# First head's maxima turned ahead of the second pair's bits, fewer fillers, and a new order table, in an attention and soft-mixture kernel

## The chip, the core and the metric

The kernel runs on one core of a Trainium2 chip. The core has five engines that work side by side, each with a queue of its own that is served strictly in order: TensorE (PE in the profile) multiplies matrices, VectorE (DVE), ScalarE (ACT) and GpSimd (POOL) work on elements, and SyncE (SP) issues transfers, which 16 DMA engines carry out. Engines wait for one another through semaphores. The metric is the device time of one execution in microseconds (us), less is better.

## The reference

Inputs are `q`, `k`, `v` of 4 batches x 8 heads x 768 tokens x 64 and a projection `proj` (64x6). Each token gets six sign bits for q and six for k; a query sees only the keys with the same six bits. The attention output goes through a soft mixture of experts.

```python
q_bits = (np.einsum('bhsd,dk->bhsk', q, proj) > 0)
k_bits = (np.einsum('bhsd,dk->bhsk', k, proj) > 0)
mask = q_bucket[:, :, :, None] == k_bucket[:, :, None, :]
scores = np.where(mask, scale * q @ k.T, -1e9)
attn = exp(scores - max(scores)); attn = attn / (sum(attn) + 1e-9)
x = (attn @ v) as 3072 tokens x 512
...
logits = x @ phi
slot_input = softmax(logits over tokens).T @ x      # 32 slots
slot_out[e] = relu(slot_input[e] @ w1[e]) @ w2[e]   # 8 experts
out = softmax(logits over slots) @ slot_out
```

## The kernel before

There are 32 heads of 768 tokens, so six tiles of 128 rows each; two heads share a batch of loads and are called a pair. For one head h the kernel does this:

- `load` brings the raw q and k of a pair into the buffer `raw` (there is one such buffer, so the next pair's load waits until all readers of the last are through). `bits` multiplies `raw` with the projection on PE, and `over` (L598) turns the products into bit rows `bt`.
- `split_hi` (ACT, L564) and `split_lo` (L568) split `raw` into a rounded part and a rest, in the buffer `w4` (`w` in the profile); for the first two pairs `split_lo` runs on POOL, later on DVE.
- `spread_y`, `spread_bits`, `spread_l` and `spread_x` bring these into one of three operand buffers `XY` by DMAs (L572) or casts (L581). Heads 0, 3, 6... use `XY_141`, heads 1, 4... `XY_142`, heads 2, 5... `XY_143`. Rows 64 to 95 of each start out as constants, zeros and ones, that `first_y` writes once.
- `smax` (L650) makes the products from which a row's maximum is taken, in banks of 512 columns; there are two such banks. `most` (L660, L663, DVE) reduces one; nine reductions make a head. `shift` (L671 to L674, DVE) makes a shift of the maximum, and `shift_rows` turns it into a row of `XY`: for head 0 by products with the identity (L685) and casts on ACT and DVE (L687, L688), for all others by a product (L691), a cast (`mr`, L694) and a DMA.
- `scores` (L706) makes the masked, shifted scores with two products, in three banks; `exps` (L712, ACT) takes the exponential of a bank, again nine to a head; `acc` (L720, L723, POOL) sums the exponentials, and `av` (L732) multiplies them with `v`.

For each pair, sums, reciprocals (`pair_rec`, L751) and the logits of the mixture (`pair_add`, L771 and L773) follow; for each batch of eight heads a running softmax (`batch_...`); and at the end two layers of experts, whose weights are loaded along the way.

`keep_warm` (L524) issues PE products that nothing reads, called fillers here. While head 0's maxima are made, `smax` issues two fillers behind each bank's last product, and eight behind the very last.

**Order.** The kernel is scheduled by hand: instructions go into each engine's queue in the order in which the program issues them. The program makes a list of steps, each with a number, sorts it and issues it. One unit of the number is one of a head's six tiles. `WHEN` has the numbers of a head in the middle, relative to the head's start; `FIRST` replaces single numbers for the first heads, and `LAST` for the last ones. So a change of these numbers moves steps on all engines at once, SP's transfers too.

Of the kernel before, what the change touches and what calls it, by code (L numbers as in the profile page):

```python
# [45 lines left out]
WHEN = {'load': -21.2267,  # L46
 'bits': -13.66,
 'split_hi': -13.5002,
 'split_lo': [-12.4984, -11.5982],
 'spread': [[-13.2693, -9.5764, -8.868, -8.1927], [-12.8094, -12.4762, -10.6553, -10.2703]],  # L50
 'load_v': [0.2058, -0.1243],
 'smax': [[-8.5643, -8.5079, -8.2213, -6.4622, -6.9729, -7.4688, -7.2277, -5.9816, -5.6736, -4.4691, -4.4083, -4.9056], [-9.6301, -9.6119, -8.9294, -8.8703, -8.072, -5.8278, -5.6254, -7.7717, -5.8098, -3.9059, -3.8333, -4.928]],
 'scores': [[0.2222, 3.1567, 4.6188, 0.8581, 0.0933, 2.3238, 2.8345, 2.9849, 4.1596, 3.8243, 4.4451, 2.0185], [0.1374, 0.8796, 1.1366, 0.6129, 2.7988, 0.7436, 1.4189, 1.4936, 3.1041, 3.407, 3.5317, 3.2581]],
 'shift': [-3.0973, -3.6413],
 'shift_rows': [-2.9069, -2.4936],
 'acc': [[5.6492, 5.6716, 7.3725, 7.9438, 13.0472], [4.136, 4.6871, 7.6692, 9.1593, 9.1679]],
 'av': [[8.0639, 8.1163, 8.2235, 8.2342, 8.2455, 8.2853], [4.6384, 5.3911, 5.4621, 5.4695, 5.5104, 5.8666]],
 'pair_sum': 17.1288,
 'pair_turn': 17.6253,
 'pair_rec': [19.1149, 18.8822, 18.8381],  # L60
 'pair_log': 17.2824,
 'pair_x': [20.0505, 21.5752],
 'pair_add': 19.4108,
 'batch_both': 20.004,
 'batch_max': 22.2214,
 'batch_exp': 22.9038,
 'batch_turn': 27.3524,
 'batch_scale': 26.8147,
 'batch_slots': 28.9459,
 'batch_weigh': 28.16,  # L70
 'batch_share': 28.3581,
 'batch_arrange': 31.3938,
 'load_weights': 20.0463,
 'most': [[-8.202, -8.0525, -6.4306, -6.7445, -6.9514, -5.8288, -5.3798, -3.6478, -4.8148], [-8.9354, -8.7621, -8.4274, -6.309, -4.4576, -7.5104, -5.212, -3.7625, -3.8958]],
 'exps': [[1.1938, 4.8483, 2.6209, 0.9684, 2.85, 3.0592, 6.3758, 5.1251, 2.7028], [0.621, 1.687, 1.3077, 3.163, 2.7312, 1.8054, 4.0071, 4.3752, 4.1145]]}

FIRST = {('load', 4): 4.5756,
 ('bits', 2): -9.2469,
 ('split_hi', 2): -4.1215,
 ('split_lo', 2, 0): -1.8302,  # L80
 ('split_lo', 2, 1): -1.4643,
 ('spread_y', 2): -0.7103,
 ('spread_bits', 2): -1.5968,
 ('spread_l', 2): 0.3263,
 ('spread_x', 2): 1.0892,
 ('smax', 1, 0, 0): -9.1254,
 ('smax', 1, 0, 1): -11.3828,
 ('smax', 1, 1, 0): -11.2936,
 ('smax', 1, 1, 1): -8.0143,
 ('smax', 1, 2, 0): -3.7459,  # L90
 ('smax', 1, 2, 1): -1.1988,
 ('smax', 1, 3, 0): -0.1767,
 ('smax', 1, 3, 1): -4.9113,
 ('smax', 1, 4, 0): -2.3094,
 ('smax', 1, 4, 1): -1.6126,
 ('smax', 1, 5, 0): -1.3265,
 ('smax', 1, 5, 1): -5.1589,
 ('first_y', 1): -25.6577,
 ('first_y', 2): -82.8016,
 ('spread_y', 1): -28.42,  # L100
 ('spread_l', 0): -16.9491,
 ('spread_bits', 1): -17.4347,
 ('bits_rest',): -25.7325,
 ('bits_copy',): -42.5516,
 ('most', 1, 0): -5.0585,
 ('most', 1, 2): -8.9264,
 ('most', 1, 3): -6.9825,
 ('most', 1, 4): -2.1518,
 ('most', 1, 6): 1.0699,
 ('most', 1, 7): -3.1409,  # L110
 ('most', 1, 8): -1.7431,
 ('most', 1, 10): 1.8611,
 ('most', 1, 11): -3.8479,
 ('bits_first', 1): -27.9402,
 ('bits', 0): -58.4653,
 ('split_hi', 0): -52.0505,
 ('split_lo', 0, 0): -26.6142,
 ('split_lo', 0, 1): -17.7524,
 ('spread_x', 0): -8.8883,
 ('load_v', 0): -5.7992,  # L120
 ('smax', 0, 0, 0): -36.0223,
 ('scores', 0, 0, 0): -7.0811,
 ('most', 0, 0): -25.23,
 ('exps', 0, 0): -6.0662,
 ('smax', 0, 0, 1): -24.9204,
 ('scores', 0, 0, 1): -3.7252,
 ('smax', 0, 1, 0): -19.0895,
 ('scores', 0, 1, 0): -3.5002,
 ('most', 0, 2): -18.6614,
 ('exps', 0, 2): -1.9816,  # L130
 ('smax', 0, 1, 1): -31.0234,
 ('scores', 0, 1, 1): -5.6082,
 ('most', 0, 3): -28.5477,
 ('exps', 0, 3): -4.5302,
 ('smax', 0, 2, 0): -27.4878,
 ('scores', 0, 2, 0): -7.1428,
 ('most', 0, 4): -24.8444,
 ('exps', 0, 4): -6.2104,
 ('smax', 0, 2, 1): -17.8184,
 ('scores', 0, 2, 1): -0.679,  # L140
 ('smax', 0, 3, 0): -16.4261,
 ('scores', 0, 3, 0): -0.1673,
 ('most', 0, 6): -14.5291,
 ('exps', 0, 6): 0.9718,
 ('smax', 0, 3, 1): -19.0487,
 ('scores', 0, 3, 1): -1.6999,
 ('most', 0, 7): -18.5753,
 ('exps', 0, 7): 1.9975,
 ('smax', 0, 4, 0): -18.101,
 ('scores', 0, 4, 0): 1.7338,  # L150
 ('most', 0, 8): -15.938,
 ('exps', 0, 8): 2.9611,
 ('smax', 0, 4, 1): -13.4653,
 ('scores', 0, 4, 1): -1.7121,
 ('smax', 0, 5, 0): -13.1733,
 ('scores', 0, 5, 0): -1.2017,
 ('most', 0, 10): -10.3631,
 ('exps', 0, 10): -1.1195,
 ('smax', 0, 5, 1): -15.1162,
 ('scores', 0, 5, 1): 0.7755,  # L160
 ('most', 0, 11): -13.5877,
 ('exps', 0, 11): 1.6535,
 ('shift', 0): -9.6249,
# [1 line left out]
 ('av', 0, 0): -0.6783,
 ('acc', 0, 1): -0.9262,
 ('av', 0, 1): 1.2278,
 ('acc', 0, 2): 4.1542,
 ('av', 0, 2): 2.8888,
 ('acc', 0, 3): 4.7925,  # L170
 ('av', 0, 3): 3.1606,
 ('acc', 0, 4): 8.0454,
 ('av', 0, 4): 3.9777,
 ('acc', 0, 5): 12.7489,
 ('av', 0, 5): 4.9168,
 ('spread_l', 1): -11.2081,
 ('spread_x', 1): -8.261,
 ('load_v', 1): -37.7236,
 ('scores', 1, 0, 0): 4.5898,
 ('exps', 1, 0): 5.0814,  # L180
 ('scores', 1, 0, 1): 4.9999,
 ('scores', 1, 1, 0): 5.0209,
 ('exps', 1, 2): 5.0485,
 ('scores', 1, 1, 1): 6.5311,
 ('exps', 1, 3): 7.2738,
 ('scores', 1, 2, 0): 4.0108,
 ('exps', 1, 4): 4.1108,
 ('scores', 1, 2, 1): 6.1313,
 ('scores', 1, 3, 0): 7.5354,
 ('exps', 1, 6): 8.8956,  # L190
 ('scores', 1, 3, 1): 5.4113,
 ('exps', 1, 7): 6.4461,
 ('scores', 1, 4, 0): 6.0575,
 ('exps', 1, 8): 6.4808,
 ('scores', 1, 4, 1): 8.5523,
 ('scores', 1, 5, 0): 8.5825,
 ('exps', 1, 10): 10.3343,
 ('scores', 1, 5, 1): 7.7148,
 ('exps', 1, 11): 9.4405,
 ('shift', 1): 1.9079,  # L200
 ('shift_rows', 1): 2.3524,
 ('av', 1, 0): 9.2796,
 ('acc', 1, 1): 10.1366,
 ('av', 1, 1): 10.7972,
 ('acc', 1, 2): 12.4825,
 ('av', 1, 2): 10.8292,
 ('acc', 1, 3): 13.171,
 ('av', 1, 3): 10.9443,
 ('acc', 1, 4): 16.6799,
 ('av', 1, 4): 11.0367,  # L210
 ('acc', 1, 5): 16.9021,
 ('av', 1, 5): 14.2599,
# [1 line left out]
 ('load_v', 2): 12.3045,
 ('smax', 2, 0, 0): 2.0338,
 ('scores', 2, 0, 0): 11.7331,
 ('most', 2, 0): 2.5309,
 ('exps', 2, 0): 12.2527,
 ('smax', 2, 0, 1): 2.9954,
 ('scores', 2, 0, 1): 15.6262,  # L220
 ('smax', 2, 1, 0): 3.2113,
 ('scores', 2, 1, 0): 15.9257,
 ('most', 2, 2): 3.5357,
 ('exps', 2, 2): 16.5105,
 ('smax', 2, 1, 1): 5.2006,
 ('scores', 2, 1, 1): 11.4302,
 ('most', 2, 3): 5.4198,
 ('exps', 2, 3): 11.7998,
 ('smax', 2, 2, 0): 5.9106,
 ('scores', 2, 2, 0): 12.2138,  # L230
 ('most', 2, 4): 6.2178,
 ('exps', 2, 4): 13.3874,
 ('smax', 2, 2, 1): 2.2592,
 ('scores', 2, 2, 1): 11.5015,
 ('smax', 2, 3, 0): 2.2693,
 ('scores', 2, 3, 0): 11.909,
 ('most', 2, 6): 4.3309,
 ('exps', 2, 6): 13.1304,
 ('smax', 2, 3, 1): 4.5227,
 ('scores', 2, 3, 1): 12.3863,  # L240
 ('most', 2, 7): 4.8456,
 ('exps', 2, 7): 13.5581,
 ('smax', 2, 4, 0): 4.6005,
 ('scores', 2, 4, 0): 16.3303,
 ('most', 2, 8): 4.8433,
 ('exps', 2, 8): 18.3449,
 ('smax', 2, 4, 1): 5.2697,
 ('scores', 2, 4, 1): 14.4321,
 ('smax', 2, 5, 0): 5.5095,
 ('scores', 2, 5, 0): 16.1037,  # L250
 ('most', 2, 10): 6.7902,
 ('exps', 2, 10): 17.4702,
 ('smax', 2, 5, 1): 7.0394,
 ('scores', 2, 5, 1): 13.4048,
 ('most', 2, 11): 7.2001,
 ('exps', 2, 11): 14.0731,
 ('shift', 2): 7.353,
 ('shift_rows', 2): 8.5764,
 ('spread_y', 3): 3.2798,
 ('spread_bits', 3): 5.3768,  # L260
 ('spread_l', 3): 6.0304,
 ('spread_x', 3): 6.6527}
# [1020 lines left out]
```

## Time and profile before

| | us |
|---|---|
| median of three runs | 495.46 |
| lowest and highest run | 493.95, 496.46 |
| the profiled execution, its own time | 495.47 |
| its span, from the first to the last instruction | 493.7 |
| PE busy | 477.1 |
| DVE busy | 358.4 |
| POOL busy | 335.0 |
| ACT busy | 264.2 |

The profile lists busy time by engine, groups of instructions by source line, the chain of work that ended last (followed back from the last instruction to what released each step), and the instructions in order of time. "Idle before <- releaser" names what ended an engine's wait. The ends of PE's products are modelled, so PE can show as busy while it in fact waits a little; how long a product really takes in a stream is best read from the chain of waits, where each piece starts when the one before it ends.

### The profile page before, as it was taken

The page shows a single profiled execution, that of the slowest core. Times are in us where ns is not written, and L with a number is a line of the kernel's source. Part 1 is how long each engine was busy: PE and PEld are TensorE (multiplying, and loading weights), DVE is VectorE, ACT ScalarE, POOL GpSimd, SP SyncE. Part 2 cuts the span into 40 slices and gives each one's busy share as a digit, 9 for nine tenths or more (in the row PEclk, how much of TensorE's full clock was granted, in tenths as well). Part 3 has the DMA queues.
Part 4 walks back from the last instruction along what each step waited for, and adds up shares of the span by engine and source line. Part 5 has one row for each costly group of instructions (what it writes and reads, how often), then busy time and mean ns, then how long its engine had stood idle before and what let it go on. Part 6 is the DMA issues. An engine that isn't in the chain of part 4 may idle for free.

```text
span 493.7 us, 8863 instructions
## 1 busy us (share of the span) xinstructions
PE 477.1 (97%) x3182; PEld 294.1 (60%) x3182; DVE 358.4 (73%) x669; ACT 264.2 (54%) x506; POOL 335.0 (68%) x205
## 2 busy tenths in 40 slices
...
GB/s 157 179 82 184 98 156 110 191 159 180 176 183 172 168 172 147 198 154 192 154 194 148 170 166 189 166 191 165 189 165 102 63 173 244 245 406 394 413 313 282
DMA packets 37455, 93.66 MB, mean 190 GB/s; under 512 B 7058, under 2 KB 13332, under 8 KB 37412
## 3 DMA queue, kind: packets, MB, share of 16 engines
...
q10 hardware_dynamic: 100, 0.08, 0.1%
q0 software_dynamic: 32, 0.07, 0.0%
HBM read 52.76 MB, written 6.29 MB: 120 GB/s over the span
## 4 chain that ended last, share of the span: by engine, by line
PE 89%; DMA 3%; DVE 3%; POOL 1%; issue 1%; ACT 1%; DVEq 0%; SPq 0%; ACTq 0%; POOLq 0%
PE st L706 27%; PE av L732 26%; PE smx L650 14%; PE qs L1211 3%; PE qh L1160 3%; PE mi L605 3%; PE mi L744 2%; PE mi L759 2%; PE mi L794 2%; DMA raw<-qk 2%; DMA XY<-w 1%; PE mi L943 1%; PE mi L779 1%; PE mi L691 1%; PE st L810 1%
## 5 line engine op out<-in xcount | busy, mean ns | idle before, releaser
L723 POOL TENSOR_TENSOR acc<-acc,pt 128x768 f32<-128x768 f32 x125 | 245.0, 1970 | 35.5 <-ACT pt L712 29.7
L712 ACT ACTIVATE pt<-st 128x512 f32<-128x512 f32 x288 | 162.6, 594 | 56.7 <-PE st L706 54.2
L706 PE MATMUL st<-XY 128*128 128x512 f32 (+1 forms) x768 | 171.0, 343 | 0.5 <-DVE XY L688 0.5
L663 DVE TENSOR_REDUCE mx<-smx 128x1 f32<-128x512 f32 x192 | 128.5, 678 | 37.7 <-PE smx L650 34.9
L706 PEld LDWEIGHTS st<-XY 128*128 128x128 f32 x768 | 120.4, 189 | 25.7 <-issue 9.6
L732 PE MATMUL av<-pt,v 128*64 128x384 f32 x768 | 133.1, 491 | 0.0
L650 PE MATMUL smx<-XY 96*128 96x512 f32 (+1 forms) x384 | 120.7, 364 | 2.8 <-DVE mx L663 2.4
L650 PEld LDWEIGHTS smx<-XY 96*128 96x128 f32 x384 | 68.2, 189 | 40.6 <-DVE mx L663 17.6
L732 PEld LDWEIGHTS av<-pt,v 128*64 128x64 f32 x768 | 51.5, 136 | 67.9 <-issue 65.3
L720 POOL TENSOR_TENSOR acc<-pt 128x768 f32<-128x768 f32 x32 | 58.3, 1821 | 33.8 <-ACT pt L712 33.6
L660 DVE TENSOR_REDUCE mx<-smx 128x2 f32<-128x512 f32 x96 | 65.6, 685 | 11.3 <-PE smx L650 10.9
L736 ACT COPY avs<-av 128x384 f32<-128x384 f32 x32 | 15.3, 479 | 83.0 <-PE av L732 83.0
L568 DVE TENSOR_TENSOR w<-raw,w 128x768 fp32r<-128x768 f32 x28 | 43.0, 1535 | 0.6 <-ACT w L564 0.6
L751 DVE RECIPROCAL sm<-sm 128x128 f32<-128x128 f32 x45 | 38.4, 909 | 0.0
L564 ACT CAST w<-raw 128x768 fp32r<-128x768 f32 x32 | 25.0, 830 | 3.2 <-DMA XY<-w 2.3
L796 DVE TENSOR_TENSOR xq<-mi,r 128x256 f32<-128x256 f32 x45 | 17.6, 419 | 10.0 <-PE mi L794 10.0
L581 ACT CAST XY<-w 64x768 fp32r<-64x768 f32 x30 | 23.5, 830 | 0.0
L598 DVE TENSOR_SCALAR bt<-mi,con 128x384 fp32r<-128x384 f32 x15 | 10.2, 677 | 13.9 <-PE mi L605 7.6
L605 PE MATMUL mi<-raw,pb 128*32 128x384 f32 x128 | 16.2, 518 | 1.1 <-DMA raw<-qk 1.1
L568 POOL TENSOR_TENSOR w<-raw,w 128x768 fp32r<-128x768 f32 x4 | 7.2, 1821 | 13.7 <-ACT w L564 12.2
L794 PE MATMUL mi<-ident,avs 128*128 128x128 f32 x90 | 14.7, 272 | 0.0
L1211 PE MATMUL qs<-w 128*32 128x256 f32 x232 | 14.6, 380 | 0.0
(168 smaller groups left out, 330.6 us busy)
## 6 DMA issues: line engine op xcount, KB each, us to landing
...
XY<-w SPq DMA_DIRECT2D x48, 384.0 KB
raw<-qk SPq DMA_DIRECT2D x32, 384.0 KB
...
```

The lines of the kernel that those rows point to most:

```text
L568: (nc.vector if h > 2 else nc.gpsimd).tensor_tensor(out=w[:, 2 * x + 1], in0=st[h]["raw"][:, x], in1=w[:, 2 * x], op=ALU.subtract)
L605: nc.tensor.matmul(pts_b[j // 2 if h == 0 else 0][32 * j:32 * j + 32, 0:HC], pb[:, 32 * (j // 2):32 * (j // 2) + 32], st[h]["raw"][:, j // ...
L650: nc.tensor.matmul(pt[:, o:o + b - a], s["Y"][0:96, 0, t * P:(t + 1) * P], s["Y"][0:96, 1, a:b], start=True, stop=True)
L660: nc.vector.tensor_reduce(out=mx[:, n - 1:n + 1], in_=s["sm_ps", n - 1].rearrange("p (a x) -> p a x", a=2), axis=AX.X, op=ALU.max)
L663: nc.vector.reduce_max(out=mx[:, n:n + 1], in_=s["sm_ps", n], axis=AX.X)
L706: nc.tensor.matmul(pt[:, o:o + b - a], x[:, 1, i * P:(i + 1) * P], x[:, 0, a:b], start=first, stop=not first)
L712: nc.scalar.activation(s["P", n // 4][:, 512 * u:512 * u + 512], s["st_ps", n - (n % 4 == 2)], AF.Exp, scale=D ** -0.5)
L720: nc.gpsimd.tensor_tensor(out=s["acc"], in0=pr[:, 0:S], in1=pr[:, S:2 * S], op=ALU.add)
L723: eng.tensor_tensor(out=s["acc"], in0=s["acc"], in1=pr[:, a * S:(a + 1) * S], op=ALU.add)
L732: nc.tensor.matmul(s["av"][64 * c:64 * c + 64, 0:HC], s["v"][:, i, :], pr[:, o + c * HC:o + (c + 1) * HC], start=(i == 0), stop=(i == NT - 1))
L751: nc.vector.reciprocal(out=rs[:, k * P:(k + 1) * P], in_=rs[:, k * P:(k + 1) * P])
L1211: nc.tensor.matmul(po[32 * j:32 * j + 32], hTs[g][:, f, 32 * j:32 * j + 32], wt[1, x, 2 * g + f // 4, j][:, (f % 4) * HM:(f % 4 + 1) * HM] ...
```

## The change

Three things are changed.

1. `first_y(1)`, the constant rows of `XY_142`, is written by two ACT copies from a broadcast column in place of two POOL memsets.
2. While head 0's maxima are made, one filler follows each bank in place of two, and the eight behind the last product become one, with five more issued by a step of their own.
3. All numbers of `WHEN`, `FIRST` and `LAST` are new. Among them: `shift_rows(0)` now comes ahead of `bits(2)`, the bits of the second pair, and the second pair's `load` comes behind `spread_x(0)`.

The number of PE products that are not fillers stays the same.

```diff
     def first_y(i):
         for x in range(2):
-            nc.gpsimd.memset(XYs[i][64:96, x].bitcast(F32), float(x))
+            dst = XYs[i][64:96, x].rearrange("p a s -> p (a s)")
+            if i == 1:
+                nc.scalar.copy(dst, (ones if x else mz_wide)[64:96, 0:1].broadcast_to([32, 2 * S]))
+            else:
+                nc.gpsimd.memset(dst.bitcast(F32), float(x))
...
         if h == 0:
-            s["smax"] = s.get("smax", 0) + 1
-            keep_warm(8 if s["smax"] == 2 * NT else 2 * (n % 4 != 1), True)
+            if n % 4 != 1:
+                keep_warm(1, True)
...
+    at(-11.05, keep_warm, 5, True)
...
- ('bits', 2): -9.2469,
+ ('bits', 2): -7.8765,
...
- ('shift_rows', 0): -8.2597,
+ ('shift_rows', 0): -10.4942,
...
- ('load', 2): -9.5805,
+ ('load', 2): -19.4862,
```

Line numbers of the changed kernel are 4 higher from `first_y` on. Three places show what the tables do.

**PE, from the end of head 0's maxima to head 0's first scores.** `smx<-XY_142` are maxima of head 1, `mi<-raw,pb` the bits of the second pair, `mi<-ident,mz` and `st<-ident,mz` the turning of head 0's row, `st<-XY_141` head 0's scores, `av<-pt_83,ones` fillers. Before:

```order
L524 MATMUL av<-pt_83,ones 32x128 x8
L650 MATMUL smx<-XY_142 128x256 x2
L605 MATMUL mi<-raw,pb 32x384 x4
L650 MATMUL smx<-XY_142 128x512
L685 MATMUL mi<-ident,mz 33x128 x4
L685 MATMUL st<-ident,mz 33x128 x2
L650 MATMUL smx<-XY_142 128x512
L706 MATMUL st<-XY_141 128x512 x6
```

And of the change:

```order
L524 MATMUL av<-pt_83,ones 32x128 x6
L689 MATMUL mi<-ident,mz 33x128 x4
L689 MATMUL st<-ident,mz 33x128 x2
L654 MATMUL smx<-XY_142 128x512
L710 MATMUL st<-XY_141 128x512 x2
L654 MATMUL smx<-XY_142 128x512
L710 MATMUL st<-XY_141 128x256 x4
L654 MATMUL smx<-XY_142 128x512
L710 MATMUL st<-XY_141 128x512 x2
L654 MATMUL smx<-XY_142 128x256
L609 MATMUL mi<-raw,pb 32x384 x4
```

The bits, which need the second pair's load, stood ahead of the turning; now four pairs of score products stand between, and the bits come later.

**POOL, from its memsets at the start to the second pair.** `w<-raw,w` is `split_lo`, `bt<-pt_81` the first pair's bit rows, `XY_142` the constant rows of change 1. Before:

```order
L568 TENSOR_TENSOR w_168<-raw,w_168 128x768
L598 TENSOR_SCALAR bt<-pt_81,con 128x384
L548 MEMSET XY_142 32x1536 x2
L568 TENSOR_TENSOR w_168<-raw,w_168 128x768
L541 CAST ident<-pt_82 128x128
```

And of the change:

```order
L572 TENSOR_TENSOR w_149<-raw,w_149 128x768 x2
L602 TENSOR_SCALAR bt<-pt_81,con 128x384
L541 CAST ident<-pt_82 128x128
L544 TENSOR_TENSOR pairs<-ident 128x64
L572 TENSOR_TENSOR w_332<-raw,w_332 128x768 x2
```

Both halves of the first pair's rest now come ahead of the bit rows, and the memsets are gone. On ACT the two copies of change 1 stand ahead of the two copies of head 0's bits (`bits_copy`, L625 before) that POOL's bit rows are made from.

**SP, around the second pair's load** (`raw<-qk`); `XY_141<-w` brings the operands of head 0, `XY_142<-w` those of head 1. Before:

```order
L572 DMA XY_142<-w_168 64x2x768
L572 DMA XY_141<-w_168 32x2x768
L572 DMA XY_142<-w_168 32x2x768
L471 DMA raw<-qk 128x768 x2
L572 DMA XY_141<-w_168 64x2x768
```

And of the change:

```order
L576 DMA XY_142<-w_149 64x2x768
L576 DMA XY_141<-w_149 32x2x768
L576 DMA XY_141<-w_149 64x2x768
L576 DMA XY_141<-w_149 32x2x768
L471 DMA raw<-qk 128x768 x2
L576 DMA XY_142<-w_149 32x2x768
```

Two transfers of head 0's operands (`spread_x(0)`) moved ahead of the load, and one of head 1's behind it.

In the middle of the kernel the order of PE stays nearly the same. On DVE, `pair_add` (before: L771, L773) moved from just ahead of a `shift` to just behind it.

More of the change, by code (lines that the diff above doesn't have):

```diff
@@ L43 @@
 C_ALL = C_FD + P
[L46 to L75, printed above, removed]
@@ L77 @@
-FIRST = {('load', 4): 4.5756,
- ('bits', 2): -9.2469,
[L79 to L163, printed above, removed]
- ('shift_rows', 0): -8.2597,
[L165 to L212, printed above, removed]
- ('load', 2): -9.5805,
[L214 to L262, printed above, removed]
```

453 lines of the change are left out of this document (333 added, 120 removed).

## The prediction

> **What bounds the kernel now.** I read first the busy time of the engines in stretches of the span (columns: stretch, its length, then busy time and number of instructions for PE, weight loads, DVE, ACT, POOL, then the clock granted to PE, DMA share, GB/s).
>
> ```profile
> 0.00:25.35 25.35, 21.79 (x124) 13.57 (x124) 12.48 (x26) 6.30 (x10) 14.06 (x15) 1.00 0.65 168
> 25.35:56.20 30.85, 28.95 (x145) 17.09 (x146) 21.50 (x34) 18.99 (x34) 22.42 (x12) 1.00 0.44 106
> 56.20:425.00 368.80, 368.80 (x2299) 229.54 (x2298) 299.33 (x548) 220.34 (x417) 292.83 (x172) 1.00 0.61 170
> ```
>
> From 56.2 to 425 us PE is busy without a gap, at full clock, and the change takes no useful product away. There a new order can add waits but hardly remove any. What can be won lies ahead of 56.2 us, where PE runs fillers and waits. So I read the chain of waits there (start, length, what ran).
>
> ```profile
> 9.41 1.65 POOL bt L598
> ...
> 11.12 2.70 POOL XY L548 x2
> ...
> 13.89 1.81 POOL w L568
> ...
> 15.95 0.11 SPq L471
> ...
> 16.11 5.55 DMA raw<-qk
> ...
> 21.70 0.84 PE mi L605 x4
> ...
> 22.97 1.01 PE mi L685 x8
> ...
> 25.35 1.66 PE st L706 x6
> ```
>
> It reads: POOL makes bit rows, memsets, then `split_lo`; only then is `raw` free and the second pair's load can go; PE stands at its bits until 21.70; behind them in the queue stand the turning of head 0's row (22.97) and its scores, which begin at 25.35. But head 0's shift was ready long before, as DVE's instructions in order of time show:
>
> ```profile
> 11.11 0.67 DVE L598 TENSOR_SCALAR XY<-mi,con 16x384 fp32r<-16x384 f32 x1
> ...
> 14.06 0.69 DVE L663 TENSOR_REDUCE mx<-smx 128x1 f32<-128x512 f32 x1 [0.29 <-PE smx L650]
> ...
> 18.00 0.69 DVE L660 TENSOR_REDUCE mx<-smx 128x2 f32<-128x512 f32 x1 [0.30 <-PE smx L650]
> ...
> 19.20 0.17 DVE L674 SCALAR_TENSOR_TENSOR mz<-mi,mz 128x6 f32<-128x6 f32 x1
> ```
>
> The last reduction ends at 18.69 and the shift at 19.37, 0.7 later. From 14.06 to 18.00 there are five reductions, each behind a wait of 0.3 for PE: a bank costs (18.00 - 14.06)/4 = 0.98, of which 0.69 is the reduction.
>
> **Term 1: head 0's scores start earlier.** What fills that 0.3 are the fillers:
>
> ```profile
> 13.95 0.62 PE L524 MATMUL av<-pt,ones 128*32 128x128 f32 x4
> ```
>
> Two fillers are 4 products and 0.62; one is 0.31. A bank then costs 0.69 and DVE sets the pace; five waits of 0.3 are about 1.5 saved. Against this stands the first edit: two ACT copies come ahead of the copies for the bit rows.
>
> ```profile
> 5.79 0.83 ACT L562 CAST XY<-raw 64x768 fp32r<-64x768 f32 x1 [0.39 <-DMA raw<-qk]
> 6.53 1.56 ACT L564 CAST w<-raw 128x768 fp32r<-128x768 f32 x2
> 8.00 0.47 ACT L625 COPY pt<-mi 64x384 f32<-64x384 f32 x1
> ```
>
> A copy of 768 columns takes 0.83, one of 384 takes 0.47; none of 1536 is in the trace. It takes no less than 0.83 and no more than 2 x 0.83 = 1.66; by the slope, 0.83 + 2 x 0.36 = 1.55, which I take, as the nearest to these rows. The two end at 6.53 + 1.56 + 3.1 = 11.2, the next copy at 11.7, and the last bits of head 0 on DVE, which wait for that copy, end near 12.35 (before: 11.11 + 0.67 = 11.78), though now with three of the nine reductions ahead of them and not one. Six remain: 0.5 until the next product is there, 6 x 0.69 = 4.1, and some 0.6 where a bank of two halves must be filled first, 17.6; the shift's 0.6 makes 18.2. At the bounds of the copy this is 16.8 and 18.4. Six fillers (1.9) run in that time and cost nothing: PE has nothing else to do until the shift is there. From the turning to the first score it took 25.35 - 22.97 = 2.4. So the first score comes at 18.2 + 2.4 = **20.6, 4.7 earlier**.
>
> What could be late in its stead? Head 0's operands are issued near 11.3, when POOL ends its second half (9.4 + 1.81), and have 9 us to land. Head 1's bit rows come later: POOL makes them from 12.2 to 13.9 (1.65), so ACT's four transfers start at 13.9 in place of 12.53.
>
> ```profile
> 12.53 3.81 ACTq L572 DMA_DIRECT2D XY<-bt  x4
> ```
>
> ```profile
> 19.75 0.51 PE L650 MATMUL smx<-XY 96*128 96x256 f32 x2
> ```
>
> They take at most 3.81, to 17.7; before, they ended at 16.34 and the first product that needs them ran at 19.75 without a wait, so they land within 3.4 of the last issue, now at 21.1 at the worst: a wait of 0 to 0.5, and I take 0. ACT is free for the turning's cast at 17.7. The second pair's load goes behind two transfers more (near 1 each to issue, by 3.81/4), at about 13.2. It took 15.95 to 21.66, 5.7; the two ahead of it are 384 and, for half the rows, 192 KB, which at the 220 GB/s of this stretch are 2.6 more:
>
> ```profile
> 19.75:25.35 5.60, 4.39 (x25) 2.19 (x24) 2.02 (x4) 0.84 (x2) 0.00 (x0) 1.00 0.98 220
> ```
>
> ```profile
> XY<-w SPq DMA_DIRECT2D x48, 384.0 KB
> ```
>
> So it lands at 21.5 at the latest; its bits stand behind 2 us of products that begin at 20.6, at 22.6.
>
> **Term 2: what PE still owes.** What products take in a stream, from the chain in the middle of the kernel:
>
> ```profile
> 72.19 0.24 PE smx L650
> ...
> 74.06 0.78 PE mi L605 x8
> 74.84 4.02 PE av L732 x24
> ...
> 80.46 0.46 PE st L706 x2
> ```
>
> 512 columns are 0.235, 256 about 0.12; a tile of `av` is 4.02/6 = 0.67. Head 1's first score is here:
>
> ```profile
> 37.61 0.73 PE L706 MATMUL st<-XY 128*128 128x512 f32 x2
> ```
>
> From 25.35 to 37.61 PE's queue holds head 0's scores (6 x 0.47 + 6 x 0.24 = 4.2), eight products of head 1's maxima (1.4), five of head 2's (0.7), a turning (0.1) and five tiles of `av` (3.4): 9.8 of work in 12.26, so 2.4 are lost. The same chain shows where:
>
> ```profile
> 27.28 0.70 DVE mx L663
> ...
> 30.80 0.80 PE av L732 x4
> ```
>
> PE waits 27.0 to 28.0 for a bank, and products cost more where kinds alternate (an `av` tile alone 0.80). In the changed order the same stretch holds 12.2: the bits (0.8) and half a us of maxima that before ran ahead of 25.35 (together 1.25), and 1.15 that before ran behind 37.61. The 1.25 must be paid; the 1.15 comes back. With the same loss of 2.4, head 1's first score comes at 20.6 + 12.2 + 2.4 = 35.2, and the gain is 4.7 - 1.25 = 3.45, **3.4**. The loss is the unknown. Without it the gain would be 5.8. It can also grow: in the changed order on ACT, the four casts of the second pair follow one another, where now they stand two and two among the exponentials:
>
> ```profile
> 27.62 1.58 ACT L564 CAST w<-raw 128x768 fp32r<-128x768 f32 x2
> ...
> 30.98 1.55 ACT L581 CAST XY<-w 64x768 fp32r<-64x768 f32 x2
> ```
>
> For 3.1 us no score bank comes free; three banks hold 1.4 of scores, and maxima and an `av` tile lie beside them (about 1.7), so the block costs 0 to 2. I take the loss of before, as the one that was measured.
>
> For the rest I take nothing: the middle keeps nearly its old order on PE, whose full queue hides any step moved on another engine (the price if not is the third rival's), and at the end a turning of expert shares moves into a stretch where PE waits anyway. The profiled execution took 495.47 (its span 493.70, 1.77 around it), beside the median of 495.46; less 3.4 makes **492.1**.
>
> **Rivals.** *The wait moves downstream* (chance 0.23): the block on ACT costs 1 to 2, or POOL, whose sums stand behind the same splits, frees a buffer late. The gain is 0 to 2.4: 493.1 to 495.5. For it: ACT's casts can't shrink. Against it: they start earlier by 3.
>
> *The lost time shrinks too* (0.11): more independent products in the queue fill the 2.4: 489.7.
>
> *The clock drops* (0.04). PE's last product ends at 484.8:
>
> ```profile
> 484.00:485.00 1.00, 0.78 (x6) 0.53 (x4) 1.00 (x2) 1.00 (x3) 0.00 (x0) 1.00 1.01 401
> ...
> 488.00:489.00 1.00, 0.00 (x0) 0.00 (x0) 0.00 (x0) 0.00 (x0) 0.00 (x0) 0.66 1.01 401
> 489.00:490.00 1.00, 0.00 (x0) 0.00 (x0) 0.00 (x0) 0.00 (x0) 0.00 (x0) 0.50 1.03 414
> ```
>
> The clock halves near 488.3, after 3.5 us of idleness, and no wait of the new start is longer than 1.5. If a low share of busy time were enough, head 0's twelve maxima would double at the worst, by 4.5 (busy time of the maxima alone, same columns without POOL):
>
> ```profile
> 8.89:18.00 9.11, 4.47 (x12) 1.97 (x12) 5.43 (x9) 0.00 (x0) 1.00 0.53 133
> ```
>
> That gives 496.6, within 0.5%. The Trainium skill ("TensorE: Matmul & The Clock Gate", "Part 1: The HAM clock gate") says that the gate falls to half rate after an idle window of about 3.4 us, which speaks against taking fillers away; this trace agrees with the 3.5, and by that rule the clock stays up here.
>
> *DVE becomes the bound in the middle* (0.07), the one that ends slower. Before, DVE has a gap there, and a bank is free ahead of its use:
>
> ```profile
> 197.96 0.69 DVE L663 TENSOR_REDUCE mx<-smx 128x1 f32<-128x512 f32 x1 [0.42 <-PE smx L650]
> ```
>
> ```profile
> 199.04 0.40 PE L650 MATMUL smx<-XY 96*128 96x512 f32 x1
> ```
>
> `pair_add` now stands between the shift and this reduction. The sum of DVE's work ahead of it stays, and I find DVE through by about 197.9, still in time. The slack is 0.42 and 199.04 - 198.65, together 0.8. If DVE came later by more, each of 15 pairs would pay the excess; from 3.4/15 = 0.23 on, the kernel is slower than before. At half a us: 492.1 + 7.5 = 499.6.
>
> *The change does not do what it says* (0.03): the load lands well after 22.6 or head 0's operands after 20.6, and PE stands where it stood: 495.5.
>
> **How the numbers follow.** The forecast, a gain of 2.5 to 5, has 0.52. A measurement of this kernel can tell about 0.5%, here 2.5 us, from no change. Faster: 0.52 + 0.11 = 0.63. Within 0.5%: 0.23 + 0.04 + 0.03 = 0.30. Slower: 0.07. The range 489.3 to 495.2 leaves out the clock and DVE, half of the last rival, and some of the first two, 0.19 in all.
>
> **What would show it.** Right: the reductions of head 0 stand 0.7 apart, the shift ends near 18.2, the first score comes near 20.6, the second pair's load is issued near 13, head 1's first score comes near 35.2, and PE has no gaps from some 53 us on. Wrong: a score that waits for operands at 21, losses between 20.6 and 35 of much more than 2.4, a granted clock below 1, or gaps on PE in every pair.

## The result and the profile after

The change makes the kernel slower: 502.27 us median of four runs (501.85 to 502.48) against 495.19 for the kernel before beside it (493.95 to 496.46). The ratio is 1.0151, 95% interval 1.0125 to 1.0176. The profiled execution's span is 500.3, 6.6 more than before. I had expected 3.4 less, so 10.0 us are to be found. Medians and ratios leave out two executions in a slower state, one of e6 (664.82) and one of the kernel before beside e9 to e12 (2636.97).

The page of the changed kernel, its span, the granted clock in 40 slices of 12.5 us, and the first line of the chain:

```profile
span 500.3 us, 8836 instructions
...
PEclk9599999999999999999999999999999999989997
...
PE 85%; DVE 7%; DMA 3%; issue 1%; ACT 1%; POOL 0%; DVEq 0%; SPq 0%; ACTq 0%
```

And of the kernel before:

```profile
PEclk9999999999999999999999999999999999999997
...
PE 89%; DMA 3%; DVE 3%; POOL 1%; issue 1%; ACT 1%; DVEq 0%; SPq 0%; ACTq 0%; POOLq 0%
```

Before, the clock row had a 9 everywhere but in the last slice. Now there is a 5 in the second slice and an 8 near 440 us, and DVE has 7% of the chain where it had 3%. The first and the third of the stretches that opened the prediction, of the changed kernel:

```profile
0.00:25.35 25.35, 22.34 (x95) 13.11 (x96) 11.42 (x25) 9.34 (x12) 11.35 (x13) 0.80 0.66 169
...
56.20:425.00 368.80, 365.30 (x2265) 225.91 (x2263) 308.74 (x542) 214.50 (x413) 289.82 (x170) 1.00 0.60 165
```

In the first the clock is 0.80 where it was 1.00; in the other PE idles for 3.5 us (368.80 - 365.30), where it had no gap.

**An account by progress.** ACT copies each head's product when its last `av` is done, so the starts of these 32 copies are milestones that both kernels share. Those of heads 2 and 29, in the instructions in order of time, before:

```profile
70.53 0.48 ACT L736 COPY avs<-av 128x384 f32<-128x384 f32 x1 [4.06 <-PE av L732]
...
409.38 0.48 ACT L736 COPY avs<-av 128x384 f32<-128x384 f32 x1 [4.06 <-PE av L732]
```

And after:

```profile
71.45 0.48 ACT L740 COPY avs<-av 128x384 f32<-128x384 f32 x1 [2.94 <-PE av L736]
...
414.51 0.48 ACT L740 COPY avs<-av 128x384 f32<-128x384 f32 x1 [3.50 <-PE av L736]
```

The changed kernel is 0.92 behind at head 2 and 5.13 behind at head 29. Between, the distance stands still or shrinks by some 0.02 a head, except for three steps, at heads 10, 18 and 26, of 1.47, 1.64 and 1.66. A last milestone is the turning of the expert shares by `fold`, before and after:

```profile
445.11 1.13 PE L1141 MATMUL mi<-fold,run_x 128*128 128x128 f32 x8 [0.30 <-DVE run_x L948]
```

```profile
452.12 1.13 PE L1146 MATMUL mi<-fold,run_x 128*128 128x128 f32 x8 [0.47 <-DVE run_x L952]
```

That is 7.01 behind; from there to the end 0.4 come back. Against the prediction of 3.4 ahead, the 10.0 are: **4.3 at the start** (0.92 + 3.4), **4.2 in the middle** (5.13 - 0.92), and **1.5 at the end** (6.6 - 5.13).

**The start.** PE in order of time, after (`av<-pt,ones` are fillers, two products to each):

```profile
10.42 0.49 PE L654 MATMUL smx<-XY 96*128 96x512 f32 x1
10.84 0.41 PE L524 MATMUL av<-pt,ones 128*32 128x128 f32 x2
11.18 0.38 PE L654 MATMUL smx<-XY 96*128 96x256 f32 x1
12.40 0.50 PE L654 MATMUL smx<-XY 96*128 96x512 f32 x1 [0.84 <-DVE XY L602]
12.84 0.41 PE L524 MATMUL av<-pt,ones 128*32 128x128 f32 x2
13.17 0.38 PE L654 MATMUL smx<-XY 96*128 96x256 f32 x1
13.48 0.41 PE L524 MATMUL av<-pt,ones 128*32 128x128 f32 x2
13.82 1.32 PE L654 MATMUL smx<-XY 96*128 96x256 f32 x3
...
18.00 0.80 PE L654 MATMUL smx<-XY 96*128 96x512 f32 x1
18.73 3.03 PE L524 MATMUL av<-pt,ones 128*32 128x128 f32 x12
21.69 1.92 PE L689 MATMUL mi<-ident,mz 128*33 128x128 f32 x8
...
25.00 0.73 PE L710 MATMUL st<-XY 128*128 128x512 f32 x2 [0.24 <-DVE XY L692]
```

From 13.82 on a product takes longer: a maximum's 512 columns 0.80 and not 0.50, eight products of the turning 1.92 and not 1.06 as before and in e7. Six fillers now last 3.03, and the turning stands behind them. The first score comes at 25.00, 0.35 ahead of before where 4.7 was expected.

### The profile page after: what moved, and what is told of

It reads as the page before. It is cut to its first block, busy times and chain, and to the rows that moved or that the text cites. A ratio compares the mean times of both kernels' runs of the same rounds, so it can differ in the third digit from the quotient of the medians.

```text
span 500.3 us, 8836 instructions
## 1 busy us (share of the span) xinstructions
PE 482.1 (96%) x3162; PEld 294.0 (59%) x3162; DVE 369.4 (74%) x669; ACT 264.0 (53%) x508; POOL 332.0 (66%) x203
## 4 chain that ended last, share of the span: by engine, by line
PE 85%; DVE 7%; DMA 3%; issue 1%; ACT 1%; POOL 0%; DVEq 0%; SPq 0%; ACTq 0%
PE st L710 26%; PE av L736 24%; PE smx L654 15%; PE qs L1216 3%; PE qh L1165 3%; DVE w L572 3%; PE mi L609 2%; PE mi L763 2%; PE mi L748 2%; PE mi L798 2%; DVE mx L667 1%; DMA XY<-mr 1%; PE mi L783 1%; PE mi L947 1%; PE mi L695 1%
## 5 line engine op out<-in xcount | busy, mean ns | idle before, releaser
L716 ACT ACTIVATE pt<-st 128x512 f32<-128x512 f32 x288 | 158.2, 595 | 73.8 <-PE st L710 72.3
L710 PE MATMUL st<-XY 128*128 128x256 f32 (+1 forms) x768 | 170.5, 343 | 0.5 <-DVE XY L692 0.2
L710 PEld LDWEIGHTS st<-XY 128*128 128x128 f32 x768 | 118.2, 189 | 17.7 <-ACT pt L716 2.7
L654 PEld LDWEIGHTS smx<-XY 96*128 96x128 f32 x384 | 65.9, 191 | 45.5 <-issue 21.6
L664 DVE TENSOR_REDUCE mx<-smx 128x2 f32<-128x512 f32 x96 | 64.8, 678 | 11.8 <-PE smx L654 10.9
L572 DVE TENSOR_TENSOR w<-raw,w 128x768 fp32r<-128x768 f32 x28 | 52.8, 1886 | 0.3 <-ACT w L568 0.2
L755 DVE RECIPROCAL sm<-sm 128x128 f32<-128x128 f32 x45 | 40.4, 926 | 0.0
L572 POOL TENSOR_TENSOR w<-raw,w 128x768 fp32r<-128x768 f32 x4 | 7.2, 1821 | 18.2 <-DMA XY<-bt 16.6
L698 ACT CAST mr<-mi 12x128 fp32r<-12x128 f32 x31 | 7.9, 254 | 16.7 <-PE mi L695 13.8
L748 PE MATMUL mi<-acc,ones 128*32 128x384 f32 x120 | 15.2, 497 | 0.0
```

The lines of the kernel that those rows point to most:

```text
L572: (nc.vector if h > 2 else nc.gpsimd).tensor_tensor(out=w[:, 2 * x + 1], in0=st[h]["raw"][:, x], in1=w[:, 2 * x], op=ALU.subtract)
L654: nc.tensor.matmul(pt[:, o:o + b - a], s["Y"][0:96, 0, t * P:(t + 1) * P], s["Y"][0:96, 1, a:b], start=True, stop=True)
L664: nc.vector.tensor_reduce(out=mx[:, n - 1:n + 1], in_=s["sm_ps", n - 1].rearrange("p (a x) -> p a x", a=2), axis=AX.X, op=ALU.max)
L710: nc.tensor.matmul(pt[:, o:o + b - a], x[:, 1, i * P:(i + 1) * P], x[:, 0, a:b], start=first, stop=not first)
L716: nc.scalar.activation(s["P", n // 4][:, 512 * u:512 * u + 512], s["st_ps", n - (n % 4 == 2)], AF.Exp, scale=D ** -0.5)
L748: nc.tensor.matmul(pt[r:r + 32, 0:HC], ones, st[h + a]["acc"][:, c * HC:(c + 1) * HC], start=True, stop=True)
```

## The experiments

The kernels that were run, by the milestones of their profiled executions (heads: against 70.53 and 409.38 of before; "half rate" is when the granted clock fell to 0.50 before 480 us, and for how long). The kernel before took 495.1, 494.56 and 494.69 (medians) beside e1 to e4, e5 to e8 and e9 to e12.

| kernel | median us | ratio to before (95%) | head 2 | head 29 | `fold` less head 29 | half rate |
|---|---|---|---|---|---|---|
| before | 495.19 | | 0 | 0 | 35.73 | none |
| changed | 502.27 | 1.0151 (1.0125 to 1.0176) | +0.92 | +5.13 | 37.61 | 13.82: 10.24, 440.49: 3.41 |
| e1 | 501.0 | 1.0106 (1.0076 to 1.0136) | -1.85 | +2.40 | 37.65 | 436.85: 3.41 |
| e2 | 494.74 | 0.9984 (0.9963 to 1.0005) | -0.81 | -0.73 | 35.71 | 13.32: 10.24 |
| e3 | 505.91 | 1.0210 (1.0180 to 1.0240) | +3.53 | +5.25 | 41.69 | 11.57: 10.24, 441.65: 6.83 |
| e4 | 499.26 | 1.0074 (1.0047 to 1.0102) | +1.07 | +1.07 | 38.25 | 435.88: 3.41, 446.12: 3.41 |
| e5 | 506.56 | 1.0225 (1.0196 to 1.0255) | -0.42 | +9.49 | 37.63 | 444.53: 3.41 |
| e6 | 494.95 | 1.0004 (0.9979 to 1.0029) | -1.85 | -1.87 | 37.66 | 433.28: 3.41 |
| e7 | 497.64 | 1.0057 (1.0037 to 1.0076) | -3.41 | +1.07 | 35.98 | none |
| e8 | 499.54 | 1.0090 (1.0066 to 1.0113) | -1.86 | +2.64 | 36.80 | none |
| e9 | 492.91 | 0.9959 (0.9938 to 0.9981) | -2.98 | -3.09 | 37.59 | 431.19: 3.41 |
| e10 | 494.64 | 0.9984 (0.9962 to 1.0006) | -3.01 | -2.52 | 36.62 | none |
| e11 | 497.06 | 1.0037 (1.0012 to 1.0062) | +1.12 | +1.18 | 35.98 | 14.23: 10.24 |
| e12 | 495.9 (one run) | | -2.71 | -2.69 | 39.22 | 431.03: 6.83 |

A row of milestones is one execution. Three executions with the same start (e7, e9, e10) differ by 0.4 at head 2. The profiled execution of before took 495.47, near the slow edge of its executions without a half rate beside the experiments (492.50 to 495.96, median 493.79), so the distances to it may flatter the other kernels by more than that.

All executions have a mean granted clock on record, which tells the half rates. Up to 480 us the profiled executions with none have a mean of 0.994 or 0.995, those with one or two windows of 3.41 at half rate 0.988 to 0.991, and those with the fall at the start 0.978 to 0.984. By this the fall at the start comes in all 28 executions of the changed kernel, e2, e3 and e11 (0.977 to 0.985) and, with 0.986 and more, in no other. And the kernel before is hit by a half rate too, though not in its profiled execution: 35 of its 67 executions beside the experiments have 0.992 or less, and their median is 495.98, against 493.79 of the others.

### The fillers back

```diff
-            if n % 4 != 1:
-                keep_warm(1, True)
+            s["smax"] = s.get("smax", 0) + 1
+            keep_warm(8 if s["smax"] == 2 * NT else 2 * (n % 4 != 1), True)
...
-    at(-11.05, keep_warm, 5, True)
```

> The changed kernel with the fillers of before: two behind each bank of head 0 (eight at the last maximum) and without the step of five ahead of the last bits. Theory A (the loss at the start is the clock: one filler per bank leaves TensorE too little to do, it falls to half rate near 14 us, and this costs 4.3 us): the clock stays at 1.0 until 40 us, head 0's first score comes at 20.5 to 22.5 in place of 25.0, and the kernel takes 498.0 (497.3 to 498.7). Rival B (the fillers cost nothing, the new order of the start is itself slow): 501.5 to 502.8, first score at 24 or later even at full clock.

The clock held, the first score came at 22.36, and head 2 is 2.77 earlier than in the changed kernel. So B falls and the clock carries most of the start's loss; the rest of the 4.3 is what the second filler costs itself (see e7). The forecast of the time missed: the median fell by only 1.3. Of seven executions the one without a half rate (0.994) took 496.86, the others (0.988 to 0.990) 499.97 to 501.78. Since this varies from one execution to the next, terms are read from milestones here.

### One filler in the order of before

The opposite edit, in the kernel before.

> The kernel before, with only its fillers changed to those of the changed kernel: one per bank, a step of five. Theory A: the clock falls to half here too between 12 and 17 us, with the old order of everything else; the first score comes at 26.5 to 29 in place of 25.35 and the kernel takes 496.5 to 499.0. Rival B: clock at 1.0 throughout the start, 494.8 to 495.7. Third case: the two constant copies on ACT, which hold the last bits of head 0 back to 12.4 us and which this kernel does not have, are needed for the fall: clock at 1.0 and 493.5 to 495.5.

The windows around the fall in this kernel:

```profile
9.91:13.32 3.41, 2.39 (x12) 1.08 (x10) 3.29 (x6) 0.00 (x0) 3.35 (x3) 1.00 0.78 187
13.32:23.56 10.24, 9.91 (x37) 4.96 (x35) 3.90 (x8) 0.00 (x0) 2.54 (x4) 0.50 0.73 182
```

The clock falls here too, without the two copies on ACT, so the third case falls. But the forecast of the time missed, since the fall costs little: the first score comes 1.0 later (26.35), and the time can't be told from before's. In the old order PE stands until 21.70 for the second pair's load at full clock, so I read the small price as slower products that fill this wait. A low clock has a price where PE is what is waited for. That head 2 is even 0.81 earlier is not shown to be the fillers' doing: the trace of before has two waits near 55 us, 1.3 together, that this one lacks (shown below, with term 2).

### Tables of before mixed in

e3 takes `WHEN` of before, e4 takes `WHEN`, `LAST` and the fillers of before.

> The changed kernel with the table WHEN of before (heads from the third on), its start and its table LAST as changed. Theory C (three steps in which a batch's shares are worked out cost 1.45, 1.4 and 1.65 us, since on VectorE two small reductions and a longer split_lo now stand ahead of the maxima): these 4.4 us go, 497.9 (497.0 to 498.8), and TensorE has no idle time between 60 and 430 us. Rival D (the loss there comes from operands that are late after the changed start): 501.5 or more.

> The changed order of the start (table FIRST) and the constant copies on ACT, with the fillers and the tables WHEN and LAST of before. If A and C hold and add up, and the half rate at the end (440.4 to 443.7 us in the changed kernel) belongs to LAST: the prediction's own 3.4 us of gain, 491.8 (490.8 to 492.8). If the start's gain is eaten downstream (rival of the prediction): 493.1 to 495.5. If B: 494 to 496.

In e3 the sums of heads 28 and 29 are inverted before they are turned, so that pair's weights are not the reference's. In both, the steps at heads 10, 18 and 26 are gone (in e4 head 2 and head 29 both stand at +1.07), so the steps belong to `WHEN`, and D falls. But neither time came out as forecast: where the new first heads meet the old `WHEN`, between heads 0 and 2, 3.2 us are lost (e4: -2.14 to +1.07). A mixed table is a third order, not a part of either; so single numbers were moved from here on.

### The steps in the middle

VectorE of the changed kernel where a batch's shares are worked out:

```profile
150.48 0.68 DVE L602 TENSOR_SCALAR bt<-mi,con 128x384 fp32r<-128x384 f32 x1
151.19 0.55 DVE L880 TENSOR_REDUCE ml<-dl 64x1 f32<-64x384 f32 x1
151.77 0.15 DVE L882 TENSOR_SCALAR run_n<-ml 64x1 f32<-64x1 f32 x1
151.97 2.60 DVE L572 TENSOR_TENSOR w<-raw,w 128x768 fp32r<-128x768 f32 x1
154.50 0.68 DVE L667 TENSOR_REDUCE mx<-smx 128x1 f32<-128x512 f32 x1
155.10 1.98 DVE L572 TENSOR_TENSOR w<-raw,w 128x768 fp32r<-128x768 f32 x1
157.00 0.68 DVE L667 TENSOR_REDUCE mx<-smx 128x1 f32<-128x512 f32 x1
```

PE's waits in all of 60 to 425 us, in the view of waits (what waited, for whom, us, times, longest):

```profile
PE smx L654 <- DVE mx L667: 2.9, 6, 0.5
```

Six waits of 0.5, two in each of three batches, and each for a maximum that stands behind a `split_lo` (L572). The first of these takes 2.60 here; in pairs without a batch it takes 1.64. Two edits, both with e1's fillers:

```diff
- 'split_lo': [-12.8124, -12.3177],
+ 'split_lo': [-12.4, -11.4],
```

> The changed kernel with the fillers of before (as in e1_fillers_back), and the two times of split_lo in WHEN put back by 0.4 and 0.9, so that on VectorE each split_lo stands behind the next maximum and not ahead of it, as before the change; TensorE's order stays. Theory C1 (the steps of 1.45, 1.64 and 1.66 us at heads 10, 18 and 26 come from the maxima that stand behind split_lo): the steps fall to 0.2 or less, head 29's product ends 2.0 to 2.4 ahead of before's, and the time is 4.0 to 4.8 under e1_fillers_back's. Rival C2 (the step comes from the two small reductions of batch_max themselves, wherever split_lo stands): the steps stay at 1.0 to 1.7.

```diff
- 'batch_max': 22.6329,
+ 'batch_max': 23.6,
```

> The changed kernel with the fillers of before, and batch_max at 23.6 in place of 22.63, so that its two small operations on VectorE stand behind the first split_lo and its maximum, and not ahead of them; split_lo stays ahead of the maxima. Theory C3 (the first split_lo takes 2.60 in place of 1.64 because the small operations shift it against GpSimd's sums, and that delay is the step): the first split_lo takes 1.64 in all pairs, and the steps fall to 0 to 0.6 each. C1: some step stays, since the maxima still stand behind split_lo and the small operations: 0.7 to 1.7 each. C2: 1.0 to 1.7 each.

e5 missed: with every maximum ahead of its `split_lo` the first one takes 1.02 to 1.05 in most pairs, but now each pair costs, some 0.8 without a batch (13 waits of PE, 6.5 us in all, for L664). I take it that this order on VectorE needs another one on PE; no run tests that. e6 hit: at heads 10, 18 and 26 the changes are -0.02, +0.16 and +0.15, and PE's six waits are gone. The same place on VectorE in e6:

```profile
147.79 0.68 DVE L602 TENSOR_SCALAR bt<-mi,con 128x384 fp32r<-128x384 f32 x1
148.38 1.71 DVE L572 TENSOR_TENSOR w<-raw,w 128x768 fp32r<-128x768 f32 x1
150.01 0.68 DVE L667 TENSOR_REDUCE mx<-smx 128x1 f32<-128x512 f32 x1
150.72 0.55 DVE L880 TENSOR_REDUCE ml<-dl 64x1 f32<-64x384 f32 x1
151.31 0.15 DVE L882 TENSOR_SCALAR run_n<-ml 64x1 f32<-64x1 f32 x1
151.38 1.21 DVE L572 TENSOR_TENSOR w<-raw,w 128x768 fp32r<-128x768 f32 x1
152.51 0.68 DVE L667 TENSOR_REDUCE mx<-smx 128x1 f32<-128x512 f32 x1
```

From the end of the bit rows to the end of the second maximum it is 4.72 and not 6.52, with the same seven instructions. Of these 1.80, 1.66 come from the two `split_lo` alone (2.92 against 4.58). Why does their length depend on their place? e12 leaves out most of GpSimd's sums (and has the fillers of before), so its time says nothing about the change:

```diff
-        elif h < BH - 1 or n < NT - 1:
+        elif h >= BH - 2 and (h < BH - 1 or n < NT - 1):
```

> The changed kernel with the fillers of before; left out are GpSimd's sums of the third to sixth product tile of every head but the last two (so the row sums are too small). Theory C4 (split_lo on VectorE is long because it has to wait for GpSimd's sums, and so its length depends on where it falls among them): split_lo takes 0.9 to 1.05 everywhere, and the steps at heads 10, 18 and 26 are under 0.3. Rival (split_lo's length has another cause, such as late casts on ACT or transfers): 1.6 and 2.0 as before, 2.6 where a batch is worked out, and steps of 1.4 to 1.7.

The groups of `split_lo`, changed kernel and e12:

```profile
L572 DVE TENSOR_TENSOR w<-raw,w 128x768 fp32r<-128x768 f32 x28 | 52.8, 1886 | 0.3 <-ACT w L568 0.2
```

```profile
L572 DVE TENSOR_TENSOR w<-raw,w 128x768 fp32r<-128x768 f32 x28 | 26.6, 951 | 0.2 <-ACT w L568 0.2
```

Without GpSimd's sums all 28 take 0.95 or 0.96 and the steps are gone (-0.03, +0.15, +0.14). So a `split_lo` waits for GpSimd's sum that is under way, up to 1.65 (2.60 - 0.95), and that wait shows as its own duration. The other traces say the same one by one: in before, the changed kernel, e1, e5 and e6, each of the 28 begins while a sum runs, and ends 0.81 to 0.87 after that sum's end. The 2.60 above begins 0.03 after a sum did: the two small reductions have moved it there.

### The start, and both repairs

e7 gives two fillers to the first three banks and two to the wait for the last bits, then one per bank as changed.

```diff
             if n % 4 != 1:
-                keep_warm(1, True)
+                s["smax"] = s.get("smax", 0) + 1
+                keep_warm(2 if s["smax"] <= 3 else 1, True)
...
+    at(-30, keep_warm, 2, True)
```

> The changed kernel with two fillers in place of one behind the first three banks, and two more in TensorE's wait for the last bits of head 0; one per bank from there, as changed. Theory A (the clock falls because the products that run fill too small a part of a window of some 3.4 us, about 40 to 50 per cent by the products' own times; at 60 it stays): the clock stays at 1.0 through the start, the first score comes at 20.6 to 21.4, head 2's product ends 2.3 to 3.6 ahead of before's (1.85 ahead in e1_fillers_back), and the time is 1.0 under to 0.3 over e1_fillers_back's. Rival: one filler per bank is too little by itself, the clock falls at 14 to 18 us, and head 2 ends 0.3 behind to 1.0 ahead of before.

PE in order of time in e7:

```profile
16.72 1.74 PE L524 MATMUL av<-pt,ones 128*32 128x128 f32 x12
18.39 1.06 PE L690 MATMUL mi<-ident,mz 128*33 128x128 f32 x8
...
20.85 0.73 PE L711 MATMUL st<-XY 128*128 128x512 f32 x2 [0.53 <-DVE XY L693]
```

The clock holds, the first score comes at 20.85, and head 2 is 3.41 ahead of before's. Nearly the same start with the clock down stands at +0.92: the clock's price is 4.33 (4.10 between e9 and e11). The time is 3.4 under e1's, more than was expected; 1.6 of it is there at head 2, the rest comes at the end, where six of seven executions of e1 have a half rate and five of ten of e7. e11 moves `batch_max` alone, e9 joins it to e7:

> The changed kernel with batch_max at 23.6 and nothing else changed: the clock still falls at the start. Theory: head 2's product 0.9 behind before's, as in the changed kernel, no step at heads 10, 18 and 26, head 29's 0.7 to 1.1 behind, and 497.7 (497.0 to 498.5). If the steps came back in another form: over 499.

> The changed kernel with the two edits that each gave back one loss: the fillers of e7_two_then_one and batch_max at 23.6 as in e6_batch_max_later; the end as changed. If the losses add up: first score at 20.9, head 2's product 3.4 ahead of before's, head 29's still 3.3 to 3.6 ahead, and 4.6 under e7_two_then_one: 493.0 (492.0 to 494.0), which beats the kernel before where the half rate at the end costs it no more than there. If something of the gain is lost between (for instance a wait that the steps hid): 494.0 to 496.0.

In both, the milestones keep their distance from head 2 to head 29 (+1.12 and +1.18; -2.98 and -3.09). The two losses add up, and e9 is 0.4% under the kernel before (0.9959, 0.9938 to 0.9981). By the medians that is 1.8 us, less than the 3.09 at head 29; among executions without a half rate it is 0.9 (492.68 and 493.62). So with both losses repaired the forecast's 3.4 is still not reached.

### The end

```diff
- ('av', -1, 4): 0.8422,
+ ('av', -1, 4): 0.1,
...
- ('av', -1, 5): 1.1546,
+ ('av', -1, 5): 0.16,
```

> The changed kernel with the fillers of before, and the last two tiles of av put at 0.1 and 0.16 in LAST, so that they run before and between the one-column products of the last head and not behind them. Theory E (the half rate near 440 us comes from 3.8 us in which only one-column products and small transposes run; where the fall is looked for in windows of 3.4 us that begin at another place in each execution, a shorter stretch is hit less often): the median falls by 0.5 to 2.0 against e1_fillers_back (501.0) and the executions spread by over 1.5 us. Rival F (the end is slow by its order and not by the clock): the clock at 1.0 at the end and no gain, or the same half rate and 500.7 to 501.3.

> The kernel of e9_start_and_batch with the table LAST of before. The stretch of one-column products and small transposes at the end is then 2.8 us long and not 3.8. Theory E (the half rate there is met by chance, less often in a shorter stretch; without it both ends take the same 84.2 us from head 29's product): head 29's product as in e9_start_and_batch, the median 0 to 1.2 under it; where no half rate falls in the profiled execution, 35.7 us from head 29's product to the turning of the shares, where it does, 37.4. Rival F (the order of LAST is slow by itself): 1.5 to 2.0 under e9_start_and_batch, half rate or not.

e8's median is 1.5 under e1's as expected and its spread 2.5, but without half rate its end still takes 36.80, 0.8 more than the unchanged order takes in e7 and e11 (35.98): the edit itself costs, and its gain can't be told from chance. e10 missed: 1.7 over e9, though no half rate falls in its profiled execution. It loses 0.7 between heads 27 and 29 and 0.6 behind; again a table that met another. Without a half rate its executions are 0.9 over e9's (493.62 and 492.68), and it is hit six times in twelve, e9 four. So E's mechanism is seen: the half rate comes in some executions of one kernel and not in others, and costs 1.4 in e7 (medians of 498.17 and 496.80). That a shorter stretch is hit less often is not shown; e10 and before rather speak against it.

## Why the prediction was wrong

**Term 1, the start: right in all but the clock.** With the clock held (e7) the shift ends at 18.19 (predicted 18.2) and the first score comes at 20.85 (predicted 20.6). The step that failed is "Six fillers (1.9) run in that time and cost nothing", and with it the reason against the clock rival, that "no wait of the new start is longer than 1.5". In the window ahead of the fall no wait is over 0.84, and the clock fell all the same. The rival's price was right in size, "by 4.5" at the worst; measured 4.33. Its parts were not: it doubled the maxima alone, and of the 4.15 that the first score loses between e7 and the changed kernel 2.0 are up to the shift's end (18.19 and 20.20), 1.3 are the fillers behind which the turning stands, and 0.9 the turning itself. Its chance, 0.04, was too low.

The windows of the changed kernel on either side of both falls:

```profile
10.41:13.82 3.41, 2.57 (x11) 1.16 (x11) 2.71 (x5) 1.59 (x3) 2.44 (x3) 1.00 0.82 189
13.82:24.06 10.24, 10.18 (x37) 5.98 (x36) 3.73 (x8) 0.42 (x1) 0.55 (x2) 0.50 0.83 213
437.08:440.49 3.41, 3.41 (x29) 2.87 (x30) 1.97 (x6) 0.48 (x1) 0.00 (x0) 1.00 0.92 354
440.49:443.90 3.41, 3.41 (x20) 1.82 (x18) 0.55 (x1) 0.48 (x1) 1.74 (x2) 0.50 1.01 394
```

PE's busy time does not give it away: ahead of the second fall it is 3.41 of 3.41. What runs there, for 2.4 of the 3.41, are one-column products and three transposes. So I counted columns, by the rows in order of time. The window from 10.41 to 13.82 has two products of 512 columns, two of 256 and six filler products of 128, some 2,300. Before, at the same place of its own window (10.45 to 13.86), PE runs this:

```profile
10.28 0.62 PE L524 MATMUL av<-pt,ones 128*32 128x128 f32 x4
11.13 0.50 PE L650 MATMUL smx<-XY 96*128 96x512 f32 x1 [0.23 <-DVE mx L663]
11.56 0.62 PE L524 MATMUL av<-pt,ones 128*32 128x128 f32 x4
12.54 0.50 PE L650 MATMUL smx<-XY 96*128 96x256 f32 x2 [0.35 <-DVE mx L663]
12.97 0.62 PE L524 MATMUL av<-pt,ones 128*32 128x128 f32 x4
13.53 0.49 PE L650 MATMUL smx<-XY 96*128 96x512 f32 x1
```

The same maxima, but ten filler products (two of the first four lie ahead of the window), some 2,800, and the clock holds. I did the same for every window of all fourteen traces from 4 us on, with each product's columns shared out over its recorded time. The 13 windows that a half rate followed while PE still had work have 940 to 2,560 columns; those at full rate that none followed have 2,530 and more. The window ahead of the changed kernel's second fall has some 2,400. Since the ends of products are modelled, the edge is good to some 200 columns.

**Term 2: right in size, by luck.** The gain of 3.4 is 3.41 at head 2 in e7 (2.98 and 3.01 with the same start in e9 and e10). But head 1's first score comes there at 36.70 and not at 35.2: the stretch holds the 12.2 of work that was counted, and the loss in it is 3.6 (15.85 - 12.2), not 2.4. What makes up for it was not in the sum. Behind that stretch the trace of before has two waits, 1.3 together, that e7 lacks:

```profile
53.19 0.50 PE L650 MATMUL smx<-XY 96*128 96x512 f32 x1 [0.35 <-DVE mx L663]
...
55.70 0.50 PE L650 MATMUL smx<-XY 96*128 96x512 f32 x1 [0.95 <-DVE mx L663]
```

e2, which has the old order too, lacks them as well, so they may belong to this one execution of before.

**The middle: "For the rest I take nothing" failed**, and in it "whose full queue hides any step moved on another engine". The steps take 4.77 (1.47 + 1.64 + 1.66), and a slow drift gives back 0.56. The rival that named VectorE (the fourth of the list, which the prediction calls its third) was right on the engine, but it priced `pair_add` over 15 pairs; what counted was `batch_max` in three, and not by its own 0.7 but by the wait that it moved `split_lo` into. I had taken the durations of a row as fixed; that of `split_lo` was 1.0 in one place and 1.97 in another already before. PE's six waits are 2.9 of the 4.77; the rest does not show as idle time, and where it lies is not shown.

**The end: taking nothing failed**, for a reason not thought of. From head 29 to `fold` it is 1.88 longer; the same order without half rate (e7, e11) takes 35.98, 0.25 more than before, so "PE waits anyway" is nearly right and 1.63 is the clock. Behind `fold`, 0.4 comes back. All four executions of the changed kernel have this fall (mean clock 0.980 or 0.981; the profiled execution of e11, without it, has 0.983), where before has a half rate in about half of its own.

Sum: 4.3 + 4.2 + 1.5 = 10.0, which is the miss.

**What stays open**: what exactly is counted, and where it decides. Columns were counted here, not varied by themselves; rows, kinds and passes of the products were not told apart. Why the end of one order is hit more often than that of another is open too: e4 has the end of before, instruction for instruction, and is hit in four executions of four, before in 35 of 67.
